# A reordered head in a fused attention and feed-forward kernel on one core

## The chip, the cores and the metric

The kernel runs on one core of one Trainium2 chip. Its engines are TensorE (PE, with its weight loads shown apart as PEld), VectorE (DVE), ScalarE (ACT), GpSimd (POOL) and SyncE (SP). The metric is the device time of one execution in microseconds (us); the median of several runs is given.

## The reference, cut to what matters

Batch 8, 8 heads, 576 positions, head size 64. Attention is causal with a decay from a running sum of log f; its output is laid out by token and goes through a feed-forward part with the gate h - tanh(h).

```python
scores = scale * np.matmul(q, k.transpose(0, 1, 3, 2))
log_f = np.log(np.clip(f, 0.0001, 1.0))
cum = np.cumsum(log_f, axis=-1)
decay = cum[:, :, :, None] - cum[:, :, None, :]
scores = np.where(causal, -1000000000.0, scores + decay)
attn = softmax(scores)                       # over keys
x = np.matmul(attn, v)                       # to tokens x (heads * head size)
h = x @ w_in                                 # 4608 x 512 @ 512 x 2048
out = (h - np.tanh(h)) @ w_out               # 4608 x 2048 @ 2048 x 512
```

## The kernel before, in words

**Operands.** Everything on TensorE is float16. q and k are kept transposed (`QT`, `KT`: head size on partitions) with three more rows: the running sum scaled, its low part, and ones or minus ones, so that one matmul of 67 rows gives score and decay together. The sums for batch 0 come from `decay_sum` (a scan on DVE over 64 rows, in two pieces), `decay_turn` (small TensorE transposes into the bank `ct`) and `decay_cols` (three DVE operations that write columns of `qa` and `ka`). For the later batches `decay_rows` computes `chi`, `cq` and `clo`, and `load_aug` copies them into `QT` and `KT` by DMAs on SP's queue.

**Batch 0, the head of the program.** It is worked by blocks of 128 queries (the fifth has 64). For a block `ib` and a half `a` of the heads, `half0` transposes q and k on TensorE (line L275, eight transposes into one PSUM bank, from the pool `ps_m` or `ps_tr`) and copies them to `QT` and `KT` (`copy0`, L286 on ACT or L288 on DVE; the letters of its last argument say which engine copies q and which k). `scores0(ib, ti)` computes a tile of 512 score columns (L303, and L306 for the mask on the diagonal) into one of two banks (`ps_sc`) and its exponential on ACT (L308). `values0` multiplies by v into the one bank pair `ps_av` (L316), `norm0` divides on DVE (L326 to L328), and `turn0` transposes the result on TensorE (L337) and copies it to `XR` on DVE (L338).

**Unread matmuls.** `spin(n)` issues n matmuls (L246) whose result nobody reads, ahead of the first transposes.

**Later batches** go through pairs of heads: `trans` turns q or k on TensorE (L257), with one copy on ACT (L264) and one on DVE (L266); `scores` (L361) has seven tiles a pair, `values` (L389) and `turn` follow. Of the feed-forward part, `step()` emits the next piece: `mlp1` (L451, L465, gate at L417 on ACT and L418 on DVE), `mlp2` (L584), `seven` (L506).

**Order.** All five queues are scheduled by hand: each engine runs its instructions in the order of the calls in the text, and an instruction waits on semaphores for what it reads or overwrites. The head is a list of calls at the end of the program; from the second batch on, `slot` deals out steps between score tiles by the table `TAKE`. Loads of q, k, v and weights are issued by POOL, with eight semaphores used in turn, so the ninth waits for the landing of the first. POOL also clears the tiles `el` and parts of `qn` and `kn`, and masks later scores (L380).

Of the kernel before, what the change touches and what calls it, by code (L numbers as in the profile page):

```python
# [8 lines left out]
FP32 = mybir.dt.float32  # L9
# [5 lines left out]
PITCH = 640  # L15
# [7 lines left out]
def kernel(  # L23
# [72 lines left out]
    def load_first(dst, src, n):  # L96
        p0 = max(0, (n + 1) * P - S)
        nc.gpsimd.dma_start(out=dst[p0:P, n, :, 0:D],
                            in_=src[0, :, n * P:(n + 1) * P - p0, :].rearrange("h p d -> p h d"))
# [14 lines left out]
    def load_v(b, n):  # L114
        load_block(vn[b % 2], v, b, n)
# [13 lines left out]
    neg16 = cst.tile([P, P], FP16)  # L129
    tri16 = cst.tile([P, P], FP16)  # L130
    ones16 = cst.tile([P, S], FP16)
    minus16 = SW[0].rearrange("p k n -> p (k n)")[0:2 * H, 0:S]
    chi = cst.tile([NH, S], FP16)
    clo = cst.tile([NH, S], FP16)
    cq = cst.tile([NH, S], FP16)
    EL = [cst.tile([P, 192], FP16, tag=f"el{i}", name=f"el{i}") for i in range(3)]
    nc.vector.memset(qa[:, :, :, D:AW], -1.0)
    nc.vector.memset(ka[:, :, :, D + 2:AW], 1.0)
    nc.vector.memset(ones16, 1.0)
# [33 lines left out]
    def decay_sum(c0, c1):  # L173
        nc.vector.tensor_tensor_scan(out=cum[:, c0:c1], data0=ones16[0:NH, c0:c1], data1=lf[:, c0:c1],
                                     initial=cum[:, c0 - 1:c0] if c0 else 0.0, op0=ALU.mult, op1=ALU.add)
# [12 lines left out]
    def decay_turn(blocks):  # L188
        if not CT:
            CT.append(ps_tr.tile([P, UW], FP32, tag="tr", name="ct"))  # L190
        for ib in blocks:
            t0 = min(ib * P, S - P)
            nc.tensor.transpose(out=CT[0][:, ib * H:(ib + 1) * H], in_=cum[0:H, t0:t0 + P], identity=id32)

    def decay_cols(b0, b1):
        ct = CT[0][:, b0 * H:b1 * H].rearrange("p (n h) -> p n h", h=H)
        hi = ka[:, b0:b1, :, D]
        nc.vector.tensor_scalar(out=qa[:, b0:b1, :, D + 2], in0=ct, scalar1=inv_qscale,
                                scalar2=-SHIFT * inv_qscale, op0=ALU.mult, op1=ALU.add)
        nc.vector.tensor_scalar_mul(out=hi, in0=ct, scalar1=inv_qscale)  # L200
        nc.vector.scalar_tensor_tensor(out=ka[:, b0:b1, :, D + 1], in0=ct, scalar=inv_qscale, in1=hi,
                                       op0=ALU.mult, op1=ALU.subtract)
# [40 lines left out]
    def spin(n):  # L243
        av = ps_av.tile([P, 2, 512], FP32, tag="av", name="spin")
        for _ in range(n):
            nc.tensor.matmul(out=av[:, 0, :], lhsT=ones16[:, 0:P], rhs=ones16[:, 0:UW])  # L246

    def trans(b, c, src, dst, eng):
        pn, g3 = S // NT6, NT6 // 2
# [18 lines left out]
    def trans0(ib, a, pool, engs):  # L268
        p0 = max(0, (ib + 1) * P - S)
        pn = P - p0  # L270
        t32 = pool.tile([P, UW], FP32, tag="tr" if pool is ps_tr else "m", name="t32")
        t16 = t32.bitcast(FP16)[0:D + 3, 0:H * pn].rearrange("p (x h n) -> p x h n", x=2, h=HH)
        for x, src in enumerate((qa, ka)):
            for h in range(HH):
                nc.tensor.transpose(out=t16[:, x, h, :], in_=src[p0:P, ib, a * HH + h, 0:D + 3],  # L275
                                    identity=id16[p0:P, p0:P])
        T0[(ib, a)] = t16, engs
# [3 lines left out]
    def copy0(ib, a, x):  # L281
        w = min(P, S - ib * P)
        t16, engs = T0[(ib, a)]
        to = (QT, KT)[x][0][:, a * HH:(a + 1) * HH, ib * P:ib * P + w]
        if engs[x] == "A":
            nc.scalar.activation(out=to, in_=t16[:, x, :, :], func=AF.Copy)  # L286
        else:
            nc.vector.tensor_copy(out=to, in_=t16[:, x, :, :])  # L288

    def half0(ib, a, pool, engs):  # L290
        trans0(ib, a, pool, engs)
        copy0(ib, a, 0)
        copy0(ib, a, 1)

    def scores0(ib, ti):
        w = min(P, S - ib * P)
        n = UW // w
        ps = ps_sc.tile([P, 512], FP32, tag="sc", name="ps")
        e = aex.tile([P, 512], FP16, tag="e", name="e")
        todo = [(h, j) for h in range(H) for j in range(ib + 1)][n * ti:n * ti + n]  # L300
        for i, (h, j) in enumerate(todo):
            at = slice(i * w, (i + 1) * w)
            nc.tensor.matmul(out=ps[:, at], lhsT=KT[0][:, h, j * P:(j + 1) * P],  # L303
                             rhs=QT[0][:, h, ib * P:ib * P + w], start=True, stop=(j < ib))
            if j == ib:
                nc.tensor.matmul(out=ps[:, at], lhsT=neg16, rhs=tri16[:, 0:w], start=False, stop=True)  # L306
            E[(0, h, j, ib)] = e[:, at]
        nc.scalar.activation(out=e, in_=ps, func=AF.Exp, scale=qscale)  # L308

    def values0(ib):  # L310
        w = min(P, S - ib * P)
        av = ps_av.tile([P, 2, 512], FP32, tag="av", name="av")
        av = av[0:w, :, 0:HH * (D + 1)].rearrange("p i (h d) -> p i h d", h=HH)
        for h in range(H):
            for j in range(ib + 1):
                nc.tensor.matmul(out=av[:, h // HH, h % HH, :], lhsT=E.pop((0, h, j, ib)),  # L316
                                 rhs=vn[0][:, j, h, 0:D + 1], start=(j == 0), stop=(j == ib))
        AV[ib] = av

    def norm0(ib):  # L320
        w = min(P, S - ib * P)
        av = AV.pop(ib)
        xn = fin.tile([P, NJ, P], FP16, tag="xn", name="xn")
        XN[(0, ib)] = xn[0:w, 0:NPAIR, :]
        rs = fin.tile([P, 2, HH, 1], FP32, tag="rs0", name="rs")[0:w]
        nc.vector.tensor_scalar_add(out=rs, in0=av[:, :, :, D:D + 1], scalar1=1e-9)  # L326
        nc.vector.reciprocal(out=rs, in_=rs)
        nc.vector.tensor_tensor(out=XN[(0, ib)].rearrange("p (i c) (a d) -> p i (c a) d", i=2, a=2),  # L328
                                in0=av[:, :, :, 0:D], in1=rs.to_broadcast([w, 2, HH, D]), op=ALU.mult)
# [271 lines left out]
    def step(n=1):  # L601
        for fn, *args in mlp[done[0]:done[0] + n]:
            fn(*args)
        done[0] += n
# [42 lines left out]
        goal[0] = base + take  # L647
        upto(goal[0])

    load_v(0, 0)  # L650
    spin(6)
    decay_sum(0, 2 * P)
    decay_turn((0, 1))
    decay_sum(2 * P, S)
    spin(1)
    decay_turn((2, 3, 4))
    decay_cols(0, 1)
    decay_cols(2, NJ)
    nc.vector.tensor_scalar_mul(out=neg16, in0=id16, scalar1=-BIG)
    half0(0, 0, ps_m, "VA")  # L660
    trans0(0, 1, ps_m, "VA")
    load_first(qa, q, 2)
    load_first(ka, k, 2)
    load_v(0, 1)
    load_first(qa, q, 3)
    load_first(ka, k, 3)
    load_v(0, 2)
    load_v(0, 3)
    load_first(qa, q, 4)
    load_first(ka, k, 4)  # L670
    load_v(0, 4)
    load_win(0, DFF // 2)
    for h in (0, 2):
        load_qk(qn, q, 1, h, h + 2)
        load_qk(kn, k, 1, h, h + 2)
    load_win(DFF // 2, DFF)
    copy0(0, 1, 0)
    copy0(0, 1, 1)
    scores0(0, 0)
    decay_cols(1, 2)  # L680
    scores0(0, 1)
    half0(1, 0, ps_m, "AV")
    half0(1, 1, ps_m, "VV")
    scores0(1, 0)
    scores0(1, 1)
    half0(2, 0, ps_m, "VV")
    scores0(1, 2)
    half0(2, 1, ps_tr, "VV")
    values0(0)
    scores0(1, 3)  # L690
    scores0(2, 0)
    norm0(0)
    scores0(2, 1)
    scores0(2, 2)
    half0(3, 0, ps_m, "VV")
    scores0(2, 3)
    half0(3, 1, ps_tr, "VV")
    values0(1)
    scores0(2, 4)
    norm0(1)  # L700
    turn0(0)
    nc.vector.memset(KT[1][:, :, S:PITCH], 0.0)
    nc.vector.memset(vn[1][D:P, NJ - 1, :, 0:D], 0.0)
    nc.vector.memset(vn[1][:, :, :, D:VW], 1.0)
    decay_rows(False)
    nc.vector.memset(minus16, -1.0)
    nc.sync.dma_start(out=QT[1][D:D + 2, :, :], in_=minus16)
    nc.sync.dma_start(out=KT[1][D + 2:D + 3, :, 0:S], in_=ones16[0:H, :])
    scores0(2, 5)
    scores0(3, 0)  # L710
    scores0(3, 1)
    half0(4, 0, ps_m, "VV")
    scores0(3, 2)
    half0(4, 1, ps_tr, "VV")
    scores0(3, 3)
    values0(2)
    norm0(2)
    scores0(3, 4)
    turn0(1)
    decay_rows(True)  # L720
    load_aug(1)
    load_v(1, 0)
    load_v(1, 1)
    for e in EL:
        nc.gpsimd.memset(e, 0.0)
    for n in range(2, NJ):
        load_v(1, n)
    load_qk(qn, q, 1, HH, H)
    load_qk(kn, k, 1, HH, H)
    for _, two in raw:  # L730
        rows = two[3 * P // 4:P, 0:TC].rearrange("p (s d) -> p s d", d=D)
        for s0, s1, by in ((NJ - 2, 2 * (NPAIR * NJ + 2), NJ), (1, 2, 1), (NJ * H, NJ * H + 3, 2)):
# [1 line left out]
    for t in range(0, NFT, 4):  # L734
        load_wout(t, t + 4)
    scores0(3, 5)
    scores0(3, 6)
    scores0(3, 7)
    scores0(4, 0)
    scores0(4, 1)  # L740
    values0(3)
    norm0(3)
    turn0(2)
    scores0(4, 2)
    step()
    scores0(4, 3)
    step()
    trans(1, 0, qn, QT, "AV")
    scores0(4, 4)
    turn0(3)  # L750
    step()
    trans(1, 0, kn, KT, "AV")
    values0(4)
    norm0(4)
    step()
    goal[0] = done[0]
    TAKE = [4, 4, 5, 5, 7, 9] + [8, 8, 8, 7, 8, 7, 8] + 4 * [8, 7, 8, 7]
# [33 lines left out]
```

## Time and profile before

| | us |
|---|---|
| median of 3 runs | 342.31 (342.2 to 342.93) |
| the profiled execution | 343.36 |
| its span, first to last instruction | 341.7 |
| PE busy | 333.2 (98%) |
| DVE busy | 237.9 (70%) |
| ACT busy | 227.2 (66%) |
| POOL busy | 160.6 (47%) |
| first unread matmul | starts at 1.87 |
| first scores of batch 0 | start at 8.61 |
| first scores of batch 1 | start at 34.35 |

Times in the profile are from the start of the span. Busy PE counts pipelined matmuls, so it isn't PE at its peak. In rows of the timeline the first number is the start, the second the length, and what stands in brackets is the idle time of that engine before it and what ended it.

### The profile page before, as it was taken

Reading aid. Unit: us, or ns where it says so; the run is one execution under the profiler, and the core shown is the slowest. Engines: PE = TensorE matmul, PEld = TensorE weight load, DVE = VectorE, ACT = ScalarE, POOL = GpSimd, SP = SyncE. Lnnn points to the kernel's source line nnn. Section 1 sums busy time; section 2 is a strip of 40 time slices with the busy share of each in tenths; the row PEclk is TensorE's granted clock in tenths of the full one; section 3 lists DMA queues with packets and bytes.
Section 4 is the critical chain, followed back from the end, with each engine's and each line's share of the span. In section 5 each row is a group of like instructions: output and inputs, shape, how many; then the busy total and the mean of one; then the engine's idle time right before and its main releaser. Section 6 shows DMA issues by size and latency. Waiting matters only on the chain.

```text
span 341.7 us, 8813 instructions
## 1 busy us (share of the span) xinstructions
PE 333.2 (98%) x3402; PEld 240.5 (70%) x3402; DVE 237.9 (70%) x493; ACT 227.2 (66%) x425; POOL 160.6 (47%) x320
## 2 busy tenths in 40 slices
PE   7999999999999999999999999999999999999995
PEld 3889776655488558888886578656877786486484
DVE  6486885648995788458854876488547865974973
ACT  4687977869854886588657865787568744624631
POOL 8966448865367727763686458652222210000000
PEclk9999999999999999999999999999999999999999
DMA  9999999999999999999999999998430013002002
GB/s 89 142 201 189 205 202 151 150 188 189 183 117 100 191 218 144 152 197 185 164 154 190 168 170 163 197 167 171 86 111 19 20 50 109 1 33 92 2 31 92
DMA packets 161867, 45.96 MB, mean 135 GB/s; under 512 B 141538, under 2 KB 160290, under 8 KB 161826
## 3 DMA queue, kind: packets, MB, share of 16 engines
q0 software_dynamic: 100160, 18.36, 79.3%
q1 hardware_dynamic: 61586, 26.99, 39.1%
q8 instruction: 26, 0.43, 0.5%
q14 instruction: 15, 0.12, 0.1%
q10 hardware_dynamic: 80, 0.07, 0.1%
HBM read 36.85 MB, written 9.44 MB: 135 GB/s over the span
## 4 chain that ended last, share of the span: by engine, by line
PE 91%; DVE 4%; ACT 3%; DMA 1%; issue 0%; ACTq 0%; DVEq 0%
PE hps L465 32%; PE cx L506 16%; PE cz L506 12%; PE ps L361 11%; PE av L389 7%; PE ops L584 4%; PE hps L451 3%; PE ps L303 2%; PE t L275 1%; ACT e L308 1%; DMA snap<-in_f_dram 1%; DVE gt L418 1%; PE t L257 1%; PE av L316 1%; DVE KT L266 1%; PE ps L306 1%
## 5 line engine op out<-in xcount | busy, mean ns | idle before, releaser
L418 DVE TENSOR_TENSOR gt<-hps,th 128x512 f16<-128x512 f32 x144 | 98.6, 688 | 46.1 <-ACT th L417 45.3
L465 PE MATMUL hps<-XR,win 128*128 128x512 f16 (+4 forms) x640 | 125.7, 336 | 0.0
L370 ACT ACTIVATE e<-ps 128x512 f16<-128x512 f32 x168 | 98.4, 595 | 34.4 <-PE ps L361 33.1
L417 ACT ACTIVATE th<-hps 128x512 f32<-128x512 f32 x144 | 86.1, 598 | 27.0 <-PE hps L465 20.7
L380 POOL TENSOR_SCALAR_AFFINE_SELECT e<-e 128x128 f16<-128x128 f16 x162 | 56.0, 346 | 102.0 <-ACT e L370 101.6
L465 PEld LDWEIGHTS <-win 128*128 128x128 f16 x640 | 56.3, 97 | 43.2
L361 PE MATMUL ps<-QT,KT 67*128 67x512 f16 (+1 forms) x336 | 68.4, 277 | 0.5 <-DVE KT L266 0.3
L506 PEld LDWEIGHTS <-gt 128*128 128x128 f16 x640 | 59.9, 97 | 9.5 <-DVE gt L418 0.4
L361 PEld LDWEIGHTS <-KT 67*128 67x128 f16 x336 | 31.9, 98 | 19.6 <-DVE KT L266 1.3
L94 POOL DMA_DIRECT2D vn<-in_v_dram x40 | 34.2, 857 | 4.8 <-DMA win<-in_moe_w_in_dram 2.5
L499 DVE TENSOR_TENSOR snap<-cz,snap 128x512 f32<-128x512 f32 x24 | 16.6, 691 | 23.3 <-ACT e L370 10.1
L506 PE MATMUL cz<-wout,gt 128*128 128x256 f16 x256 | 32.0, 272 | 0.0
L389 PEld LDWEIGHTS <-e 128*128 128x128 f16 x784 | 28.0, 97 | 3.1
L389 PE MATMUL av<-vn,e 128*128 128x65 f16 x784 | 29.2, 193 | 0.0
L506 PEld LDWEIGHTS <-sw 128*128 128x128 f16 x256 | 24.0, 97 | 4.5
L506 PE MATMUL cx<-kn,gt 128*128 128x256 f16 x192 | 25.7, 272 | 0.0
L397 DVE TENSOR_TENSOR xn<-av,rs 128x640 f16<-128x640 f32 x28 | 23.1, 825 | 1.0
L105 POOL DMA_DIRECT2D qn<-in_q_dram x25 | 21.3, 853 | 1.1 <-issue 1.1
L105 POOL DMA_DIRECT2D kn<-in_k_dram x25 | 21.3, 852 | 0.6 <-issue 0.6
L543 ACT ACTIVATE snap<-cx 128x512 f32<-128x512 f32 (+1 forms) x18 | 9.9, 549 | 16.7 <-PE cx L506 16.7
L308 ACT ACTIVATE e<-ps 128x512 f16<-128x512 f32 x25 | 14.4, 596 | 5.3 <-PE ps L306 3.4
L451 PE MATMUL hps<-XR,win 128*128 128x256 f16 x128 | 16.6, 272 | 0.3 <-DVE gt L418 0.3
(106 smaller groups left out, 376.3 us busy)
## 6 DMA issues: line engine op xcount, KB each, us to landing
vn<-in_v_dram POOLq DMA_DIRECT2D x32, 128.0 KB, 7.1
out_dram<-snap SPq DMA_DIRECT2D x16, 256.0 KB
qn<-in_q_dram POOLq DMA_DIRECT2D x24, 128.0 KB, 5.6
kn<-in_k_dram POOLq DMA_DIRECT2D x24, 128.0 KB, 4.3
QT<-TQ SPq DMA_DIRECT2D x10, 288.0 KB
KT<-TK SPq DMA_DIRECT2D x10, 288.0 KB
out_dram<-ost SPq DMA_DIRECT2D x11, 256.0 KB
win<-in_moe_w_in_dram POOLq DMA_DIRECT2D x2, 1024.0 KB, 11.3
```

The costliest lines, as they stand in the source:

```text
L94: nc.gpsimd.dma_start(out=dst[0:pn, n, h0:h1, 0:D], in_=src[b, h0:h1, n * P:n * P + pn, :].rearrange("h p d -> p h d"))
L105: nc.gpsimd.dma_start(out=to, in_=src[b, :, n * P:n * P + pn, :].rearrange("h p d -> p h d"))
L361: nc.tensor.matmul(out=ps[:, col:col + n], lhsT=KT[b % 2][0:D + 3, h, j * P:(j + 1) * P], rhs=QT[b % 2][0:D + 3, h, i0:i0 + n], start=True ...
L370: nc.scalar.activation(out=e[:, lo:hi], in_=ps[:, lo:hi], func=AF.Exp, scale=qscale)
L380: nc.gpsimd.affine_select(out=view, in_=view, compare_op=ALU.is_ge, fill=0.0, base=0, pattern=pat, channel_multiplier=-1)
L389: nc.tensor.matmul(out=av[:, a, ib, :], lhsT=E.pop((b, 2 * c + a, j, ib)), rhs=vn[b % 2][:, j, 2 * c + a, 0:D + 1], start=(j == 0), stop=( ...
L397: nc.vector.tensor_tensor(out=xn.rearrange("p i (a d) -> p a i d", a=2), in0=av[:, :, :, 0:D], in1=rs.to_broadcast([P, 2, NJ, D]), op=ALU. ...
L417: nc.scalar.activation(out=th, in_=hps, func=AF.Tanh, scale=-1.0)
L418: nc.vector.tensor_tensor(out=to, in0=view(hps), in1=view(th), op=ALU.add)
L451: nc.tensor.matmul(out=hps[:, w * SB:(w + 1) * SB], lhsT=win[:, ci, ft * P:(ft + 1) * P], rhs=XR[:, ci, t * SB:(t + 1) * SB], start=(ci == ...
L465: nc.tensor.matmul(out=hps[:, o:o + n], lhsT=win[:, ci, ft * P:(ft + 1) * P], rhs=XR[:, ci, t:t + n], start=(ci == 0), stop=(ci == NCH - 1))
L506: nc.tensor.matmul(out=ps, lhsT=stationary(u, LHS[ph], ft, m), rhs=moving(RHS[ph], ft), start=fresh and ft == 0, stop=(ft == HF - 1), skip ...
```

## The change

It touches the head of the program and `spin`, and adds `quarter0`. The bodies of all other functions stay.

- `spin` reads a small tile `one128`, which is the first memset on DVE, and its 512 columns are the same 128 read four times. There are ten unread matmuls in place of seven: eight at the start, one before q's and one before k's first transposes.
- The columns of the sums for blocks 0 and 1 are made right after their two transposes; the second scan and `neg16` come after them on DVE. The other three blocks' columns are made between the two score tiles of block 0.
- For the first four heads of block 0, q and k are transposed into a bank each (`quarter0`), and copied by DVE and ACT.
- The loads stand in one list ahead of the work: q and k of blocks 2 and 3 before any v, v of blocks 0 to 2, q and k of block 4, and the rest of v. Batch 1's v is loaded in halves of heads (ten loads in place of five), and q and k of its upper heads by two heads (four loads in place of two), all ahead of the fills of `el`, `qn` and `kn` and of `wout`.
- `values0(0)` moves from before `scores0(1, 3)` to after `scores0(2, 3)`, `values0(1)` to after `scores0(2, 5)`; the turns, the rows of the sums for batch 1, the fills for batch 1 and the first steps move with them. `trans` of batch 1's k moves from before `values0(4)` to after `norm0(4)`.

```diff
+    one128 = cst.tile([P, 1, P], FP16)
...
+    nc.vector.memset(one128, 1.0)
     nc.vector.memset(qa[:, :, :, D:AW], -1.0)
...
-            nc.tensor.matmul(out=av[:, 0, :], lhsT=ones16[:, 0:P], rhs=ones16[:, 0:UW])
+            nc.tensor.matmul(out=av[:, 0, :].rearrange("p (a n) -> p a n", n=P), lhsT=one128[:, 0, :],
+                             rhs=one128.to_broadcast([P, UW // P, P]))
...
+    def quarter0(ib, a, x, eng):
+        t32 = ps_m.tile([P, UW], FP32, tag="m", name="t32")
+        t16 = t32.bitcast(FP16)[0:D + 3, 0:HH * P].rearrange("p (h n) -> p h n", h=HH)
+        for h in range(HH):
+            nc.tensor.transpose(out=t16[:, h, :], in_=(qa, ka)[x][:, ib, a * HH + h, 0:D + 3], identity=id16)
+        to = (QT, KT)[x][0][:, a * HH:(a + 1) * HH, ib * P:(ib + 1) * P]
+        if eng == "A":
+            nc.scalar.activation(out=to, in_=t16, func=AF.Copy)
+        else:
+            nc.vector.tensor_copy(out=to, in_=t16)
```

The head before:

```python
    load_v(0, 0)
    spin(6)
    decay_sum(0, 2 * P); decay_turn((0, 1)); decay_sum(2 * P, S)
    spin(1)
    decay_turn((2, 3, 4)); decay_cols(0, 1); decay_cols(2, NJ)
    # neg16
    half0(0, 0, ps_m, "VA"); trans0(0, 1, ps_m, "VA")
    # loads: q, k 2; v 1; q, k 3; v 2, 3; q, k 4; v 4; half of win; four of batch 1's q, k; half of win
    copy0(0, 1, 0); copy0(0, 1, 1)
    scores0(0, 0); decay_cols(1, 2); scores0(0, 1)
    half0(1, 0, ps_m, "AV"); half0(1, 1, ps_m, "VV")
    scores0(1, 0); scores0(1, 1); half0(2, 0, ps_m, "VV"); scores0(1, 2); half0(2, 1, ps_tr, "VV")
    values0(0); scores0(1, 3); scores0(2, 0); norm0(0); scores0(2, 1); scores0(2, 2)
    half0(3, 0, ps_m, "VV"); scores0(2, 3); half0(3, 1, ps_tr, "VV")
    values0(1); scores0(2, 4); norm0(1); turn0(0)
    # fills for batch 1; decay_rows(False); two DMAs of constant rows
    scores0(2, 5); scores0(3, 0); scores0(3, 1); half0(4, 0, ps_m, "VV"); scores0(3, 2); half0(4, 1, ps_tr, "VV")
    scores0(3, 3); values0(2); norm0(2); scores0(3, 4); turn0(1)
    # decay_rows(True); load_aug(1); batch 1's v, q, k; fills of el, qn, kn; wout
    scores0(3, 5); scores0(3, 6); scores0(3, 7); scores0(4, 0); scores0(4, 1)
    values0(3); norm0(3); turn0(2)
    scores0(4, 2); step(); scores0(4, 3); step(); trans(1, 0, qn, QT, "AV"); scores0(4, 4); turn0(3); step()
    trans(1, 0, kn, KT, "AV"); values0(4); norm0(4); step()
```

The head after:

```python
    # all loads up to batch 1's q, k: q, k 2, 3; v 0 to 2; q, k 4; v 3, 4; win; batch 1 with v by halves
    spin(8)
    decay_sum(0, 2 * P); decay_turn((0, 1)); decay_cols(0, 2); decay_sum(2 * P, S)
    # neg16
    spin(1); quarter0(0, 0, 0, "V"); spin(1); quarter0(0, 0, 1, "A"); half0(0, 1, ps_m, "VV")
    scores0(0, 0); decay_turn((2, 3, 4)); decay_cols(2, NJ); scores0(0, 1)
    half0(1, 0, ps_m, "VA"); half0(1, 1, ps_m, "VV")
    scores0(1, 0); scores0(1, 1); half0(2, 0, ps_m, "VV"); scores0(1, 2); half0(2, 1, ps_tr, "VV")
    scores0(1, 3); decay_rows(False); scores0(2, 0); scores0(2, 1)
    half0(3, 0, ps_m, "VV"); scores0(2, 2); half0(3, 1, ps_tr, "VV"); scores0(2, 3)
    values0(0); norm0(0); scores0(2, 4); decay_rows(True); scores0(2, 5)
    values0(1); norm0(1); scores0(3, 0); turn0(0)
    scores0(3, 1); half0(4, 0, ps_m, "VV"); scores0(3, 2); half0(4, 1, ps_tr, "VV")
    scores0(3, 3); turn0(1); values0(2); norm0(2); scores0(3, 4)
    # minus16; two DMAs of constant rows; load_aug(1); fills for batch 1; fills of el, qn, kn; wout
    scores0(3, 5); turn0(2); scores0(3, 6); scores0(3, 7); scores0(4, 0); scores0(4, 1)
    values0(3); norm0(3)
    scores0(4, 2); scores0(4, 3); step(); scores0(4, 4); step(); trans(1, 0, qn, QT, "AV"); turn0(3); step()
    values0(4); norm0(4); trans(1, 0, kn, KT, "AV"); step()
```

More of the change, by code (lines that the diff above doesn't have):

```diff
@@ L648, in slot @@
         upto(goal[0])
[L650 to L668, printed above, removed]
+    for n in (2, 3):
+        load_first(qa, q, n)
+        load_first(ka, k, n)
+    for n in range(3):
+        load_v(0, n)
     load_first(qa, q, 4)
     load_first(ka, k, 4)
-    load_v(0, 4)
+    for n in (3, 4):
+        load_v(0, n)
     load_win(0, DFF // 2)
@@ L676 @@
     load_win(DFF // 2, DFF)
-    copy0(0, 1, 0)
-    copy0(0, 1, 1)
+    for h in (0, HH):
+        for n in range(NJ):
+            load_block(vn[1], v, 1, n, h, h + HH)
+        load_qk(qn, q, 1, HH + h // 2, HH + h // 2 + 2)
+        load_qk(kn, k, 1, HH + h // 2, HH + h // 2 + 2)
+    spin(8)
+    decay_sum(0, 2 * P)
+    decay_turn((0, 1))
+    decay_cols(0, 2)
+    decay_sum(2 * P, S)
+    nc.vector.tensor_scalar_mul(out=neg16, in0=id16, scalar1=-BIG)
+    spin(1)
+    quarter0(0, 0, 0, "V")
+    spin(1)
+    quarter0(0, 0, 1, "A")
+    half0(0, 1, ps_m, "VV")
     scores0(0, 0)
-    decay_cols(1, 2)
+    decay_turn((2, 3, 4))
+    decay_cols(2, NJ)
     scores0(0, 1)
-    half0(1, 0, ps_m, "AV")
+    half0(1, 0, ps_m, "VA")
     half0(1, 1, ps_m, "VV")
@@ L688 @@
     half0(2, 1, ps_tr, "VV")
+    scores0(1, 3)
+    decay_rows(False)
+    scores0(2, 0)
+    scores0(2, 1)
+    half0(3, 0, ps_m, "VV")
+    scores0(2, 2)
+    half0(3, 1, ps_tr, "VV")
+    scores0(2, 3)
     values0(0)
-    scores0(1, 3)
-    scores0(2, 0)
     norm0(0)
[L693 to L697, printed above, removed]
+    scores0(2, 4)
+    decay_rows(True)
+    scores0(2, 5)
     values0(1)
-    scores0(2, 4)
     norm0(1)
+    scores0(3, 0)
     turn0(0)
[L702 to L710, printed above, removed]
     scores0(3, 1)
@@ L715 @@
     scores0(3, 3)
+    turn0(1)
     values0(2)
@@ L718 @@
     scores0(3, 4)
-    turn0(1)
-    decay_rows(True)
+    nc.vector.memset(minus16, -1.0)
+    nc.sync.dma_start(out=QT[1][D:D + 2, :, :], in_=minus16)
+    nc.sync.dma_start(out=KT[1][D + 2:D + 3, :, 0:S], in_=ones16[0:H, :])
     load_aug(1)
-    load_v(1, 0)
-    load_v(1, 1)
+    nc.vector.memset(KT[1][:, :, S:PITCH], 0.0)
+    nc.vector.memset(vn[1][D:P, NJ - 1, :, 0:D], 0.0)
+    nc.vector.memset(vn[1][:, :, :, D:VW], 1.0)
     for e in EL:
         nc.gpsimd.memset(e, 0.0)
[L726 to L729, printed above, removed]
     for _, two in raw:
@@ L736 @@
     scores0(3, 5)
+    turn0(2)
     scores0(3, 6)
@@ L742 @@
     norm0(3)
-    turn0(2)
     scores0(4, 2)
-    step()
     scores0(4, 3)
     step()
+    scores0(4, 4)
+    step()
     trans(1, 0, qn, QT, "AV")
-    scores0(4, 4)
     turn0(3)
     step()
-    trans(1, 0, kn, KT, "AV")
     values0(4)
     norm0(4)
+    trans(1, 0, kn, KT, "AV")
     step()
```

## The prediction

> **What bounds the kernel now.** The page comes first: TensorE is busy nearly throughout, and the chain that ended last is almost all its own.
>
> ```profile
> PE 333.2 (98%) x3402; PEld 240.5 (70%) x3402; DVE 237.9 (70%) x493; ACT 227.2 (66%) x425; POOL 160.6 (47%) x320
> PE 91%; DVE 4%; ACT 3%; DMA 1%; issue 0%; ACTq 0%; DVEq 0%
> ```
>
> So a time is won or lost only where PE stands or runs below its rate. The windows of PE (us from:to, length, busy, count, granted clock, DMA share, GB/s) show where.
>
> ```profile
> 0.00:8.60 8.60, 6.06 (x28) 1.00 1.19 89
> 8.60:14.00 5.40, 5.21 (x48) 1.00 2.25 143
> 14.00:28.00 14.00, 12.63 (x252) 1.00 1.38 190
> 28.00:36.00 8.00, 8.00 (x132) 1.00 1.82 183
> ```
>
> 48 matmuls take the 5.4 us to 14.0, 252 the next 14. The timeline of PE says why: four 128-column transposes start 0.107 us apart at 13.63 ((0.61 - 0.29, one alone) / 3) and 0.06 apart from 14.06 ((0.40 - 0.22) / 3). The granted clock is 1.00 in both; the doubling is read from the spacing alone.
>
> ```profile
> 13.63 0.61 PE L275 MATMUL t<-id,qn 128*67 128x128 f16 x4
> 14.06 0.40 PE L275 MATMUL t<-id,kn 128*67 128x128 f16 x4
> ```
>
> Third, the timeline up to the first scores: KT's copy waits for QT's from the same bank, the scores for KT's copy.
>
> ```profile
> 6.16 0.19 DVE L198 TENSOR_SCALAR qn<-ct 128x8 f16<-128x8 f32 x1 [0.58 <-PE ct L193]
> 7.96 0.59 ACT L286 ACTIVATE KT<-t 67x512 f16<-67x512 f16 x1 [2.12 <-DVE QT L288]
> 8.61 0.29 PE L303 MATMUL ps<-QT,KT 67*128 67x128 f16 x1 [0.29 <-ACT KT L286]
> ```
>
> Fourth, the hand-over to batch 1, where the change moves the transposes of k:
>
> ```profile
> 31.69 0.42 PE L257 MATMUL t<-id,kn 96*128 96x96 f16 x6
> 32.04 1.45 PE L316 MATMUL av<-vn,e 128*64 128x65 f16 x40
> 33.42 1.05 PE L451 MATMUL hps<-XR,win 128*128 128x256 f16 x8
> 34.35 0.39 PE L361 MATMUL ps<-QT,KT 67*128 67x512 f16 x1
> 32.38 0.81 ACT L264 ACTIVATE KT<-t 64x576 f16<-64x576 f16 x1
> 33.48 0.81 DVE L266 COPY KT<-t 64x576 f16<-64x576 f16 x1
> ```
>
> KT's two copies, one after the other, end at 34.29; the values and the first-layer step cover them, and PE starts the scores at 34.35 having lost almost nothing.
>
> The sum is made on the profiled execution: 343.36 us, span 341.7 and 1.7 around it. The median of the runs is 342.31, 1.05 less; I take that off at the end.
>
> **1. First scores: -0.8.** The sums' columns for blocks 0 and 1 wait for two transposes of the sums (done at 5.02) and no longer for all five: 6.16 becomes about 5.1. The second scan (0.88) and neg16 (0.37) move behind them on DVE, and QT's copy behind those, at about 7.1: 5.1, three column steps to 5.6, 6.4, 6.8. k's transposes can't go before k lands: by 6.84 at the latest, where they start now without a wait; the bound below is q's start, 6.40. Four transposes end at 6.9 to 7.5, KT's copy (0.59, own bank, no wait for QT) at 7.5 to 8.1. So the first scores start at 7.6 to 8.15 in place of 8.61; I take 7.8.
>
> **2. Ten unread matmuls, not seven: +0.2.** They start after one short memset on DVE, at about 1.1 in place of 1.87 (the first DVE row is at 0.92; fills of 80 and 160 elements take 0.12 and 0.19). Eight at the spacing of 0.43 end at 4.5, under the wait for the first scan (done at 4.59). Of the two before k, one lies under the columns, one may hold k's transposes by half of itself: 0 to 0.43. Their operand reads 128 columns four times; no row has that. With the same 512 columns per instruction I take 0.43; at twice that the eight would end at 8.0 and cost about 0.5.
>
> **3. Full rate sooner: -1.0.** Cut back from 14.0 into stretches of 3.4 us, PE streams about 3.0 us of the last (10.5 to 14.0: 12 scores and masks, some 18 transposes, one gap at 12.2), 2.9 of the one before and 2.1 of the one before that; only the fullest was followed by the doubling. After the change 7.1 to 10.5 holds about 3.2 (gaps only at 7.7 and 8.7), 3.7 to 7.1 about 2.8 (gaps of 0.1 to 0.2 around the sums, q and k). So I take 10.5. The work then in 10.5 to 14.0 streams for about 3.0 us and would take 1.5; the copies between (ACT 0.59, DVE 0.42) don't shorten, and about 1.0 arrives. Bounds: 0 (still at 14.0), and -2.0 (at 7.1: the scores and transposes of 7.1 to 10.5 halve too).
>
> The Trainium skill, "TensorE: Matmul & The Clock Gate", Part 1, has full rate follow about 4 us of sustained matmuls, ±0.5; here the unread ones began at 1.87, their columns ran out at 4.4, and it came at 14.0, so the trace does not follow the rule from the first matmul. The same page, Part 4, says that transposes don't count as activity in the same way, which speaks against this part, since transposes fill 5.5 to 7.7. By the first rule the sum would hold -2.0 or more here, by the second 0.
>
> **4. Order of blocks 1 to 3: +0.8.** Block 1's first copies are DVE's 0.42 and then ACT's 0.59 from one bank (now ACT's, then DVE's); PE has them covered by the next four pairs of transposes, all but 0.5 (12.0 to 12.5). At full rate these transposes take 0.43 less: +0.3. values0(1) now follows values0(0) with two score tiles (0.5 us of PE) between. There is one av bank, freed by norm0(0), whose three steps run 15.97 to 17.08, 1.1 us: a wait of 0.6. turn0(2) comes right behind norm0(2), with one score tile (0.3) between: a wait of 0.8. They take the place of waits that PE has there now:
>
> ```profile
> PE ps L303 <- ACT e L308: 0.8, 3, 0.4
> PE ps L303 <- DVE clo L179: 0.2, 1, 0.2
> ```
>
> ACT's exponentials run on meanwhile, so about 0.9 of the 1.4 is only moved: +0.5. Bounds of the part: 0 to +1.7.
>
> **5. k of batch 1 behind values0(4): +1.1.** PE does values0(4) first (32.04 to 33.42, 1.38), then the transposes (0.35), then the step (0.87), then the scores. Transposes, ACT's copy, DVE's copy, three hand-overs: 0.42 + 0.81 + 0.81 + 0.2 = 2.2; less 0.25 that PE issues in and 0.87 of cover: 1.1 us of PE standing, where now it is 0.06. DVE also has norm0(4) (1.05) ahead of that copy, but it runs during ACT's copy. Bounds +0.8 to +1.4.
>
> **6. Loads: 0.** q and k of block 3 move four issues (0.88 each) forward; no DMA ends a wait of PE now, so there is nothing to win. Block 0's v comes 3.5 us later: issued at 9.1, median 7.1 to landing (128 KB rows), 16.2; first read at about 17.5: cover 1.3, and what is lacking of it would cost PE as much. Batch 1's v in ten halves and q, k in four for two are seven more issues on POOL of about 0.75 (the rows of two-head loads); the bytes and their order are the same. What queues behind them: the loads take eight semaphores in turn, so POOL stands until the eighth load before has landed, as this row shows
>
> ```profile
> 31.87 0.75 POOL L209 DMA_DIRECT2D wout<-in_moe_w_out_dram  x1 [2.53 <-DMA win<-in_moe_w_in_dram]
> ```
>
> so now v's second half waits for win, and the fills of el (0.7), of qn and kn (1.6) and wout stand behind: el done at 31.6 + 7 x 0.7 + 0.5 = 37.0, where ACT first writes it at 37.6; wout's first at 39 in place of 31.9. Its bytes land at about 44 as now, since the queue is what it waits for; L584 reads it from 48.3, the fourth part from 54. Cover 0.6 and 3 us. The rows for batch 1's decay leave SP about 2 us later, last at 29, read at 34.3: covered.
>
> Sum: -0.8 + 0.2 - 1.0 + 0.8 + 1.1 = +0.3; 343.36 + 0.3 - 1.05 = 342.6 us.
>
> **Rivals.** A, full rate by 7: part 3 gives -2.0, and the total is -0.7: 341.6. For it: unread matmuls without a gap from 1.1 to 4.5, and short gaps after; against: 4.4 us of activity from 1.87 did not do it. The first rule of the page is this case, and goes by its chance; 0.27. B, slower: full rate no sooner than now, since the stretches with transposes were not enough before; part 3 gives 0, total +1.3: 343.6. It decides if 128-column spacing at 11 us is still 0.107; 0.14. C, POOL: el's fills or wout arrive late. If POOL waits 1.5 us more for landings, ACT's el stands 0.9 and PE with it behind two score banks: 343.5; 0.10. D, the stall of part 5 isn't there because DVE and ACT are ahead: 341.8; 0.04. E, the change does not do what it says (the unread matmuls end at 8): 343.1 to 344; 0.03.
>
> **How the numbers follow.** Forecast 0.42, its own range 342.0 to 343.2 (parts 1, 2, 4, 5 by their bounds). 0.2% is about what a measurement of this kernel tells from no change: 341.63 to 342.99. Faster: half of A, three quarters of D, a twentieth of the forecast: about 0.2, rounded up to 0.22 for the spread. Same: 0.44 from three quarters of the forecast and half of A. The rest, 0.34, is B, C, E and the forecast's upper end. A, B and C lie between 341.5 and 343.7.
>
> **What would show it.** First scores at 7.8; 128-column spacing 0.06 from about 10.5; PE idle about 1.1 us before the first L375 (scores of batch 1) for DVE's KT; el's fills by 37 and no wait of ACT for them; PE after 60 us as before. Wrong if: full rate before 8 (A), at 14 (B), a wait of ACT for POOL near 37 (C), or scores of batch 1 without a stall (D).

## The result, and the profile after

The changed kernel takes 347.33 us (median of 4 runs, 346.46 to 348.83) where the kernel before takes 342.34 beside it (342.2 to 342.93). The ratio is 1.0147, 95% interval 1.011 to 1.0184: 5.0 us slower, outside the predicted 341.5 to 343.7. The profiled execution of the changed kernel took 346.46 with a span of 344.8, that is 3.1 more than the profiled one of before. It is the shortest of its four, and the one of before lies 1.0 above its median, so the profiles show less of the loss than the medians.

These are the page's busy line and the chain that ended last, of the changed kernel. PE has no more work than before, but transfers now stand in the chain with 5% where they had 1%:

```profile
PE 332.7 (96%) x3405; PEld 239.3 (69%) x3405; DVE 239.6 (69%) x492; ACT 226.6 (66%) x424; POOL 164.8 (48%) x327
PE 85%; DMA 5%; DVE 4%; ACT 2%; issue 1%; POOL 1%; ACTq 0%; POOLq 0%
```

These are the windows of PE (length, busy, count, granted clock, DMA share, GB/s). Up to 14 us more is done than before (117 instructions for 76); then the granted clock is 0.88 where it was 1.00, and from 28 on PE stands 1.2 us in 8:

```profile
0.00:8.60 8.60, 6.33 (x43) 1.00 1.20 90
8.60:14.00 5.40, 4.59 (x74) 1.00 2.23 142
14.00:28.00 14.00, 12.23 (x231) 0.88 1.37 188
28.00:36.00 8.00, 6.83 (x110) 1.00 1.48 163
```

These are PE's waits up to 90 us (total, times, longest). The first was forecast. POOL's masks and wout's transfer end no wait of PE in the kernel before:

```profile
PE ps L375 <- DVE KT L269: 1.2, 1, 1.2
...
PE av L403 <- POOL e L394: 1.0, 2, 0.6
PE ops L598 <- DMA wout<-in_moe_w_out_dram: 0.9, 1, 0.9
```

POOL's timeline says why. The second half of v waits 4.32 us for win and then takes five issues; q, k, the fills and only then wout stand behind it, at 39.72 in place of 31.87. Later a load waits for wout, and three masks, which PE needs, stand behind the loads:

```profile
32.60 3.63 POOL L94 DMA_DIRECT2D vn<-in_v_dram  x5 [4.32 <-DMA win<-in_moe_w_in_dram]
...
37.43 0.72 POOL L739 MEMSET el<- 128x192 f16 x3
...
39.72 3.02 POOL L211 DMA_DIRECT2D wout<-in_moe_w_out_dram  x4
...
55.99 0.89 POOL L94 DMA_DIRECT2D vn<-in_v_dram  x1 [1.62 <-DMA wout<-in_moe_w_out_dram]
...
58.87 0.90 POOL L394 TENSOR_SCALAR_AFFINE_SELECT e<-e 128x128 f16<-128x128 f16 x3
```

What the transfers moved meanwhile is the last figure of POOL's windows; first before, then after:

```profile
34.00:36.00 2.00, 1.06 (x2) 1.00 1.64 193
36.00:38.00 2.00, 1.11 (x3) 1.00 1.29 204
38.00:40.00 2.00, 1.14 (x3) 1.00 1.24 209
40.00:42.00 2.00, 0.57 (x1) 1.00 1.25 208
```

```profile
34.00:36.00 2.00, 2.00 (x4) 1.00 1.30 102
36.00:38.00 2.00, 2.00 (x6) 1.00 1.42 98
38.00:40.00 2.00, 1.94 (x8) 1.00 0.96 135
40.00:42.00 2.00, 2.00 (x4) 1.00 0.22 27
```

From 34 to 42 POOL is busy almost without a gap, and the queue runs dry: half a block of v, 64 KB, each 0.73 us (3.63 / 5) is 90 GB/s, and during the fills nothing is issued. Less was also left in the queue when POOL could go on: of the eight loads that may be under way, the seven behind win's second half have landed by 35.76 in this trace, and by 39.35 in that of before, where most of them are twice as large. In these 8 us 113 GB/s less are moved on average (203.5 against 90.5), 0.9 MB, or 4.4 us at 205 GB/s. By the trace wout's four parts land at 45.5, 48.9, 51.8 and 55.7, where they landed at 41.8, 44.4, 46.9 and 49.8.

Where PE lost its time is summed from the trace: the distance of each matmul's start to the next one's, less its columns at 2.4 per ns and 2.5 ns, by stretch (us). These two fit the trace of before, where matmuls that follow without a gap start 0.216 us apart with 512 columns, 0.109 with 256 and 0.056 with 128. Half clock counts as loss here. before_halves and v_whole are experiments below. Each row is one execution: v_whole's was the shortest of its twelve, so differences of about 1 us between the rows are within the spread.

| | 0-14 | 14-30 | 30-36 | 36-60 | 60-100 |
|---|---|---|---|---|---|
| before | 6.97 | 3.36 | 0.38 | 1.74 | 0.30 |
| after | 5.11 | 4.73 | 1.67 | 3.30 | 1.13 |
| v_whole (after, whole loads) | 4.88 | 3.39 | 1.76 | 1.34 | 0.30 |
| before_halves (before, halves) | 6.02 | 3.34 | 0.77 | 5.17 | 1.73 |

After less before is 3.19; the first matmul starts 0.73 sooner (1.14 for 1.87), and three more of 512 columns add 0.65: 3.1, the difference of the spans.

### The profile page after: what moved, and what is told of

It is laid out like the page before. It is cut to its first block, busy times and chain, and to the rows that moved or that the text cites. A ratio compares the mean times of both kernels' runs of the same rounds, so it can differ in the third digit from the quotient of the medians.

```text
span 344.8 us, 8818 instructions
## 1 busy us (share of the span) xinstructions
PE 332.7 (96%) x3405; PEld 239.3 (69%) x3405; DVE 239.6 (69%) x492; ACT 226.6 (66%) x424; POOL 164.8 (48%) x327
## 4 chain that ended last, share of the span: by engine, by line
PE 85%; DMA 5%; DVE 4%; ACT 2%; issue 1%; POOL 1%; ACTq 0%; POOLq 0%
PE hps L479 32%; PE cx L520 16%; PE cz L520 12%; PE ps L375 10%; PE av L403 6%; DMA vn<-in_v_dram 4%; PE ops L598 2%; PE hps L465 2%; PE ps L317 1%; DMA kn<-in_k_dram 1%; ACT e L384 1%; PE av L330 1%; PE t L278 1%; DVE xn L342 1%; DVE gt L432 1%
## 5 line engine op out<-in xcount | busy, mean ns | idle before, releaser
L94 POOL DMA_DIRECT2D vn<-in_v_dram x45 | 37.2, 837 | 13.6 <-DMA win<-in_moe_w_in_dram 8.8
L403 PE MATMUL av<-vn,e 128*128 128x65 f16 x784 | 29.9, 193 | 1.2 <-POOL e L394 1.0
L598 PE MATMUL ops<-wout,gt 128*128 128x512 f16 x64 | 16.4, 378 | 0.9 <-DMA wout<-in_moe_w_out_dram 0.9
```

The costliest lines, as they stand in the source:

```text
L94: nc.gpsimd.dma_start(out=dst[0:pn, n, h0:h1, 0:D], in_=src[b, h0:h1, n * P:n * P + pn, :].rearrange("h p d -> p h d"))
L403: nc.tensor.matmul(out=av[:, a, ib, :], lhsT=E.pop((b, 2 * c + a, j, ib)), rhs=vn[b % 2][:, j, 2 * c + a, 0:D + 1], start=(j == 0), stop=( ...
L598: nc.tensor.matmul(out=ops, lhsT=GT[(u, ft, m)], rhs=wout[:, ft, :], start=(ft == 0), stop=(ft == NFT - 1))
```

## The experiments

Each was timed beside the kernel before on the same chip. Before's median there was 343.28 for k_early, v_whole, fill and spins8, 343.0 for whole_k, before_halves, fills_early and whole_k_turn, 342.91 for wout_first and the two light ones, and 342.95 for few_loads. Each ratio is to those runs of before. The changed kernel itself was timed beside a before of 342.34, so a difference to it is given by the medians, and by the two ratios where these say something else.

**v_whole: the cut of batch 1's loads, in part 6, undone.** The new order of batch 0's loads stays.

```diff
-    for h in (0, HH):
-        for n in range(NJ):
-            load_block(vn[1], v, 1, n, h, h + HH)
-        load_qk(qn, q, 1, HH + h // 2, HH + h // 2 + 2)
-        load_qk(kn, k, 1, HH + h // 2, HH + h // 2 + 2)
+    for n in range(NJ):
+        load_v(1, n)
+    load_qk(qn, q, 1, HH, H)
+    load_qk(kn, k, 1, HH, H)
```

> The changed kernel with batch 1's v loaded in five whole blocks and the upper q and k in one load each, as in the kernel before, at the place where the changed kernel has its sixteen loads... of them fourteen in halves. Theory: the seven more loads push wout's issue from 31.9 to 39.7 because the eighth load behind win's second half waits for it, and that late wout costs the 0.94 us at 55.7, the 0.64 at 59.2 and the 0.40 at 67.5 with what else is lost between 54 and 68, 2.6 us in all. Expected: first wout load issued near 32, last landed near 50, no wait of PE for wout, 2.3 to 2.8 us less. Rival: the bytes set the landing and not the issue (as the prediction had it), so wout still lands at 55 and under 0.5 us is won.

342.91 us, ratio to before 0.9999 (0.9985 to 1.0013): 4.4 less than the changed kernel by the medians, 5.1 by the two ratios. wout is issued from 32.5 and landed by 50.4, the queue moves 177, 195, 209 and 205 GB/s in the four windows above, and no wait of PE for wout or for masks is left up to 90 us. The theory holds, and more is won than the 2.6 that the waits of one profile add up to. In the profiles 1.3 of the difference lies at 14 to 30 us, where the changed kernel's clock falls; in v_whole's twelve executions the mean granted clock is 0.999 to 1.0.

**before_halves: that cut alone, on the kernel before, with the fills behind the loads.**

```diff
-    load_v(1, 0)
-    load_v(1, 1)
+    for h in (0, HH):
+        for n in range(NJ):
+            load_block(vn[1], v, 1, n, h, h + HH)
+        load_qk(qn, q, 1, HH + h // 2, HH + h // 2 + 2)
+        load_qk(kn, k, 1, HH + h // 2, HH + h // 2 + 2)
     for e in EL:
         nc.gpsimd.memset(e, 0.0)
-    for n in range(2, NJ):
-        load_v(1, n)
-    load_qk(qn, q, 1, HH, H)
-    load_qk(kn, k, 1, HH, H)
```

> The kernel before with nothing but the order and cut of batch 1's last loads: v in ten halves of heads, upper q and k in four loads for two, el's fills behind them. Theory: eight loads in flight are all that POOL can have, half as large they leave the DMA queue dry, and wout's four parts land 5 to 6 us later than before's 41.8 to 49.8; PE waits for them and then for masks that stand on POOL behind waiting loads: 2 to 4 us slower than before, with full rate and head as before. Rival: it is the changed head that needs the loads sooner; before's own head has room, and under 0.7 us is lost.

346.83 us, ratio 1.0137 (1.0104 to 1.0171), 3.8 slower by the medians and 4.7 by the ratio. The head is that of before; wout is issued at 40.7 and its last part lands at 57.0. PE's waits from 30 to 90 us begin with

```profile
PE ps L361 <- ACT el L370: 1.0, 1, 1.0
PE av L389 <- POOL e L380: 0.8, 2, 0.5
PE ps L361 <- ACT e L370: 0.8, 2, 0.5
```

Here ACT does wait for el's fills, 2.29 us, and PE for ACT behind it; no wait of PE for wout is in the list. In the stretch around that wait PE streamed 44%, and the clock falls to half from 42.13 to 45.55. The fall is not the price: the two executions that kept a clock of 1.0 took 346.71 and 346.96. So the cut loads cost about 4 to 5 us in either head, by other waits each time: undoing them and doing them alone agree in size.

**wout_first: as many small loads, wout ahead of the second half of v.**

```diff
-    for h in (0, HH):
+    def load_half(h):
         for n in range(NJ):
             load_block(vn[1], v, 1, n, h, h + HH)
-        load_qk(qn, q, 1, HH + h // 2, HH + h // 2 + 2)
-        load_qk(kn, k, 1, HH + h // 2, HH + h // 2 + 2)
+    load_half(0)
+    for h in (HH, HH + 2):
+        load_qk(qn, q, 1, h, h + 2)
+        load_qk(kn, k, 1, h, h + 2)
...
     for t in range(0, NFT, 4):
         load_wout(t, t + 4)
+    load_half(HH)
```

> The changed kernel, all loads in halves as they are, but the second half of v behind wout instead of ahead of it (the upper q and k stay ahead). Fourteen small loads as before, so it tells their number from wout's place. Theory: POOL issues 64 KB each 0.75 us (85 GB/s) behind win where the queue moves 205 GB/s, and wout's 512 KB each stand behind five of those; put ahead, wout lands within 2 us of its old times, PE waits for nothing there, and 3 to 4.4 us of the changed kernel's 4.4 come back: 343 to 344.3. Rival: the number of issues is what costs, wherever they stand (the eight semaphores); then POOL is late for the next loads and masks instead, and less than 2 us come back: over 345.3.

352.44 us, ratio 1.0259 (1.0223 to 1.0296): 5.1 more than the changed kernel by the medians, 3.8 by the ratios. Half of the theory held: wout landed at 42.7 to 51.9 and PE did not wait for it. But POOL's timeline and, in the second fence, PE's show the rival's price:

```profile
52.77 0.67 POOL L215 DMA_DIRECT2D qn<-in_q_dram  x1 [3.00 <-DMA wout<-in_moe_w_out_dram]
...
55.36 0.91 POOL L394 TENSOR_SCALAR_AFFINE_SELECT e<-e 128x128 f16<-128x128 f16 x3
```

```profile
55.71 0.49 PE L403 MATMUL av<-vn,e 128*128 128x65 f16 x3 [6.92 <-POOL e L394]
```

A load goes out only when the eighth before it has landed (the loads' semaphores come round in eights). Five more in the queue made batch 2's loads wait on POOL, among them one 3.00 us for wout and one, at 54.64, 1.19 for v, and the masks stood behind these loads, in order. PE stood 6.92 us, and the clock fell to half from 53.32 to 60.14 behind that. So the extra loads delayed what followed on POOL, masks that did not read their data.

**fills_early: POOL's fills into its wait for win.** The `memset` of `EL` and of the rows of qn and kn go between the two halves.

> The changed kernel with POOL's fills (el, and the rows of qn and kn, 2.3 us together) ahead of the second half of v's loads, where POOL stands 4.3 us waiting for win, and no longer between the last load and wout. Theory (dry queue): wout is issued 2.2 us sooner, lands about 2 us sooner (last part 53.5 for 55.7), ACT's wait for el cannot come, and 1.0 to 2.2 us of the 4.4 is won. Rival 1: number of loads and the cap of eight alone set it, the fills are hidden: under 0.4 us. Rival 2: the fills between were all of it: 3.5 us or more.

347.32 us, 1.0144 (1.0117 to 1.017), as the changed kernel: rival 1. In its profile win landed 2.2 us later than in the changed kernel's, wout was issued at 39.65 all the same, and the queue moved 76, 74 and 91 GB/s from 34 to 40. So the fills between are no part of the price that the times show. As win was late in this profile, it can't show by itself what earlier fills give; it does show the queue dry with no fills between the small issues and wout.

**k_early: part 5 undone in the changed kernel.** `trans(1, 0, kn, KT, "AV")` stands before `values0(4)` again.

> The changed kernel with one line moved back: the transposes of k for batch 1's first pair stand ahead of values0(4) again. Theory: the 1.17 us in which PE stands before the first scores of batch 1 (35.06) is ACT's and DVE's copies of KT, nothing else; it falls under 0.2 and the time falls by 1.0 to 1.2 us. Rival: POOL's late fills and loads set the pace there anyway, so the stall is only moved to the next wait (el, or wout at 55.7), and the time falls by less than 0.4 us.

347.48 us, 1.0135 (1.0116 to 1.0153): nothing won. In its profile 0.3 of the 1.2 us before the first scores is left. PE's waits from 30 to 90 us now have one for el, which the changed kernel's list has not: the scores come sooner, and ACT waits 2.41 us for POOL's fill of el. Masks and wout stay:

```profile
PE av L403 <- POOL e L394: 1.2, 3, 0.5
PE ps L375 <- ACT el L384: 1.1, 1, 1.1
...
PE ops L598 <- DMA wout<-in_moe_w_out_dram: 0.5, 1, 0.5
```

**fill: PE kept busy where it waits for norm0(2).** Three unread matmuls of 512 columns ahead of turn0(2)'s transposes.

```diff
-    def turn0(ib):
+    def turn0(ib, fill=0):
...
         x32 = ps_m.tile([P, UW], FP32, tag="m", name="x32")
+        for _ in range(fill):
+            nc.tensor.matmul(out=x32.rearrange("p (a n) -> p a n", n=P), lhsT=one128[:, 0, :],
+                             rhs=one128.to_broadcast([P, UW // P, P]))
...
-    turn0(2)
+    turn0(2, 3)
```

> The changed kernel with three more unread matmuls of 512 columns ahead of the transposes of turn0(2), into the same bank that these write, where PE stands 0.65 us waiting for norm0(2). The output is the same. Theory: the granted clock falls to half at 24.30 for 3.41 us because PE streamed only about half of the 3.41 us before; filled to about 70% it stays at 1.00, and the time falls by about 1.7 us for the 0.0 to 0.1 that the three cost. Rival: the fall has nothing to do with PE's filling (a limit that full rate from 3.8 meets after some 20 us); then it comes at about 24.3 again, and the time is the same or 0.1 us longer.

347.63 us, 1.0135 (1.0111 to 1.0159). The windows of PE, first of the changed kernel, then of this one:

```profile
20.88:24.30 3.42, 2.31 (x47) 1.00 1.21 202
24.30:27.71 3.41, 3.35 (x65) 0.50 1.20 211
```

```profile
20.88:24.30 3.42, 2.95 (x54) 1.00 1.19 204
24.30:27.71 3.41, 3.35 (x88) 1.00 1.23 209
```

The clock does not fall there, as the theory has it. Over the executions, the mean granted clock is 0.999 to 1.0 in five of six here and 0.988 to 0.995 in all nine of the changed kernel and k_early. But it is also 0.999 to 1.0 in all twelve of v_whole, which has the same wait for norm0(2) and no late loads; in k_early's profile it falls at 40.24, after the wait for el. So the falls go with the late loads at least as much as with this hole, and which of them it is stays open. Nothing is won at the end either: PE comes sooner and waits longer, 1.9 us for wout and 1.4 for masks. k_early and fill say the same: while wout's last part lands at 56 to 57, what is gained ahead of it is worth nothing.

**spins8: parts 2 and 3 alone, on the kernel before.** `one128`, its memset first on DVE, the new form of `spin`, and `spin(8)` for `spin(6)`.

> The kernel before with nothing but the changed kernel's unread matmuls: the operand of 128 columns set first on DVE, eight in place of six (and the one later, of the same form). Theory: the earlier and denser start alone opens full rate at 3.8 in place of 14.1. Worked from the rates, that is worth 2.0 to 2.8 us less the 0.4 us for more matmuls where they hold the first scores, so 1.5 to 2.5 us faster than before; if a stretch of 3.41 us then falls to half filled, the clock falls again and 1.7 of it is lost. Rival: the changed order of the head opens it and not the matmuls, full rate still comes at 14, and the time is that of before or 0.4 longer.

343.35 us, 1.0012 (0.9987 to 1.0037): no gain that the times show. In its profile full rate comes at 5.01, but the clock records fall to half again from 8.42 to 11.84, after a stretch in which PE streamed 45% of the time.

**whole_k, whole_k_turn: is there a faster version?** v_whole with k's transposes back before values0(4), and the same with `turn0(2)` behind `scores0(3, 6)`.

> The changed kernel with both undone: batch 1's v, q and k in whole loads, and the transposes of k ahead of values0(4). With whole loads alone PE stood 1.2 us for DVE's KT at 31 us in its profile, and nothing that is late stands behind it any more. Theory: now the stall is the bound there, and moving the transposes back wins 1.0 to 1.2 us against whole loads alone (342.9), so 341.7 to 342.0 where before is 343.3. Rival: POOL or a score bank takes the stall over as it did with the late loads (where moving them back won nothing), and the time stays at 342.6 to 343.0.

> As the kernel with whole loads and k moved back, and turn0(2) one score tile later, so that 0.3 us more of PE's work stands between norm0(2) and the transposes that wait for it (0.65 us in the changed kernel's profile). Theory: the wait falls by about 0.25 and 0.1 to 0.3 us is won against that kernel, since the exponentials partly take the wait over; the stretch of 3.41 us there is filled a few per cent more, so the clock falls to half in fewer runs. Rival: the wait is only moved to the next score tile's bank, 0.0.

343.14 us (1.0011, 0.9992 to 1.0029) and 343.32 (1.0015, 0.9994 to 1.0037): the rival, both times. In the profile of the second PE has lost 2.1 us less than before by 60 us; then DVE waits for a transfer, and PE for DVE (0.40 us for gt at 87.62). DVE's timeline:

```profile
81.00 0.43 DVE L455 TENSOR_TENSOR qn<-wout,t 128x512 f16<-128x512 f16 x1 [1.25 <-DMA TQ<-qn]
```

PE loses 1.16 us between 72 and 100 us, where before loses 0.14. But the two profiles are no fair pair: this one was taken at 342.24, 1.1 below its median, and that of before at 343.36, 1.0 above. So much of the 2.1 may be spread between executions and no gain.

**before_light, whole_k_turn_light: less to transfer.** Both leave out the loads of v for batches 2 and 3.

> The kernel before without the loads of v for batches 2 and 3 (the old values stand in their place), that is 1.18 MB less on the queue between 50 and 88 us. A control for the next kernel. In before's profile PE waits for no transfer between 60 and 100 us, so both theories expect no change, within 0.5 us of before.

> The kernel with whole loads, k moved back and turn0(2) one tile later, without the same loads of v for batches 2 and 3. Its head lost 2.0 us less up to 60 us than before's in the profiles, and 1.0 of that was lost again between 72 and 100 us, behind operations that wait for transfers. Theory: the queue sets the pace of 60 to 90 us and gives back what the head wins; with less on it the head's gain arrives: 1.0 to 2.0 us faster than the control, and no loss between 60 and 100. Rival: the head's gain is not there in most runs (the clock opens or falls at other times from run to run): within 0.5 us of the control.

343.2 (1.0001, 0.9973 to 1.0029) and 342.33 (0.9977, 0.9951 to 1.0003). The loss between 72 and 100 us is gone (0.14), and the medians differ by 0.87, but the intervals overlap: between theory and rival, not decided. In these two profiles the head up to 60 us won only 0.3. That transfers take back the head's gain is seen in one profile and not shown by the times.

**few_loads: four loads fewer than before.** On whole_k_turn: batch 1's lower q and k in one load each, wout in two of 1 MB.

> The kernel with whole loads, k moved back and turn0(2) one tile later, and four loads fewer than before has: batch 1's lower q and k in one load each of four heads (two each before), wout in two loads of 1 MB in place of four of 512 KB. Same bytes, same order. Theory: each load costs POOL its place among eight in flight, so with four fewer the loads behind are issued sooner, the queue has more ahead of it between 30 and 55 us, and what that kernel lost between 72 and 100 us (1.0 us in its profile, behind operations that wait for transfers) is gone: 0.5 to 1.2 us faster than it (343.3), 342.1 to 342.8, under before's median. Rival: the queue itself is full there and the issues were not late; within 0.4 us of it. A second rival: 1 MB parts land later as a whole than their first halves did, and PE waits for wout's first part near 47 us: slower by up to 1 us.

343.6 us (1.0023, 0.9988 to 1.0058), and 342.95 without its longest run of 348.71: not faster. In its profile PE waits 1.3 us for wout, as the second rival had it, and the loss at 72 to 100 is gone. No version that does all the work beats the kernel before.

## Why the prediction was wrong, by its steps

**Part 6 is the step that failed: 0 forecast, 3.8 to 5.1 measured** (before_halves and v_whole, by medians and by ratios). Its list of what queues behind what was right (wout at 39 forecast, 39.72 measured; el done at 37.0, 38.15 measured). Wrong was the sentence that wout's "bytes land at about 44 as now, since the queue is what it waits for". In the trace of before the four parts land from 41.8 to 49.8, and the queue was then full (203.5 GB/s). Here it moved 90.5, with issues of 90 GB/s and less left from before, and the last part landed 5.9 us later. Rival C had the place, POOL, and priced it at 1 us. It counted neither the dry queue nor the masks, which stand behind waiting loads on the same engine. Its own sign, a wait of ACT for el, is not in the changed kernel's list, since part 5's stall has ACT write el only at 38.11; it comes in k_early and before_halves. That "the bytes and their order are the same" is no price of 0 when the issues carry half as much each. How the price divides between late wout, el, the masks and the clock stays open: it does so differently in each profile, and taking one of them away alone won nothing (wout_first the late wout, fills_early the fills in between, fill the fall of the clock).

**Part 1** forecast first scores at 7.8, the trace has 7.54, through the forecast's chain: two sums first, q's transposes at 5.27, k's when k lands (6.33), KT's copy, scores. PE's timeline:

```profile
5.27 0.41 PE L297 MATMUL t<-id,qn 128*67 128x128 f16 x4
...
6.47 0.38 PE L297 MATMUL t<-id,kn 128*67 128x128 f16 x4 [0.57 <-DMA kn<-in_k_dram]
...
7.54 0.23 PE L317 MATMUL ps<-QT,KT 67*128 67x128 f16 x1 [0.24 <-ACT KT L300]
```

**Part 2**: the eight start at 1.14 and end at 4.35; the operand read four times costs nothing extra (0.427 apart at half rate), so rival E is excluded.

**Part 3**: rival A came about, sooner than it said. In the first fence line the four transposes are 0.06 apart at 5.27, and the trace's clock records have full rate from 3.82, not 10.5. What was held against A was misread: the unread matmuls of before stream from 1.87 to 4.43, that is 2.6 us and not 4.4. Parts 1 to 3 together gave 1.6 in the forecast; 0.73 (start) less 0.65 (more matmuls) plus 1.86 (loss up to 14 us) is 1.94. This is against one profile of before; with before's head and old unread matmuls full rate came at 4.59 in before_halves, so some runs of before have part of the gain as well, and spins8 shows none in the times. What the forecast did not have is the way back: half clock from 24.30 to 27.71, 1.7 us, after 3.41 us of which PE streamed 51%.

**Part 4** was mis-sized. The waits are where it said, 0.46 for norm0(0) (forecast 0.6) and 0.65 for norm0(2) (0.8), but before lost as much in other waits there: from 14 to 30 us 3.39 in v_whole against 3.36. Its +0.5 for these waits was 0.0; its +0.3 for block 1's copies lies before 14 us, inside the 1.86.

**Part 5** stood as forecast, 1.17 us for 1.1, at the same copy of DVE. What it costs at the end is another matter: taking it away won nothing, with late loads (k_early) or without (whole_k against v_whole).

**The sum of parts 1 to 5** was +0.3, and v_whole, which has them and the new order of batch 0's loads, is at -0.4 by medians and at 1.000 within 0.15% by the ratio. The rest is part 6. Rival D's 341.8 does not follow from the sum, which gives 341.5 without part 5.

## What to carry to other kernels

Where an engine issues loads in order with a fixed number in flight, cutting loads smaller is not free although the bytes stay: compare KB per issue over issue time with the rate of the queue, and look at who stands behind on that engine. A wait that is removed ahead of a late transfer wins nothing; look first for the transfer that everything must meet. And a part that counts on 3 us of cover has to be priced with the change's own queue, not with the one in the trace of before.

## What the runs showed of the hardware that was not expected

The clock records name full rate from between 3.82 and 6.11 us in ten of eleven profiles with the new unread matmuls, and 13.68 in the other; with the old ones 14.08, 12.95 and once 4.59. Full and half rate last multiples of 3.41 us in these records, and where such stretches start differs from run to run. How full a stretch is can be worked out as its columns at the rate of the moment. Half rate ended after a stretch that unread matmuls streamed to 75% or more, and not after one of 68%. Of the stretches with many transposes one of 88%, 50 of them transposes, ended it and one of 86% did not, so transposes count here. Full rate ended, for 3.41 us or twice that, after stretches of 51, 47, 45, 44, 42, 33 and 0%, and after none of 52% or more. But two of 51% did not end it, nor did one of 45% in fill, from 59.95. So the falls lie at about half and less, and these runs show no sharp limit. The Trainium skill, "TensorE: Matmul & The Clock Gate", Part 1, has a free-running window of that length, which the 3.41 us here agree with, and names about 4 us to open, ±0.5; counted from the first matmul, the 2.7 to 12.5 us here are a wider spread. It has half rate return after an idle window of about 3.4 us; here it returned in the changed kernel with no idle gap over 0.65 us in the window, so a half-filled one can be enough.
